# Channel mixes with 64-row contractions in pairs, and other places for the adds of x, in a convolution with a phase mixer

## The chip, the cores and the metric

The kernel runs on one core of a Trainium2 chip. The metric is the time of one execution on the device in microseconds (us). TensorE (PE in the profile, PEld for its weight loads), VectorE (DVE), ScalarE (ACT), GpSimd (POOL) and SyncE (SP) each run their own queue in order and wait for one another by semaphores; DMAs are issued from the queues of SP, ACT and POOL.

## The reference

```python
# x: (8, 4224, 192), weight: (8 heads, 7 taps); w_theta, w_ch: (192, 192); w_tok_r, w_tok_i: (4224, 4224)
w = softmax(weight, axis=-1)
x = causal convolution of x over the tokens, head h of 24 channels with the taps w[h]
theta = x @ w_theta
zr, zi = x * cos(theta), x * sin(theta)
y = einsum('ts,bsd->btd', w_tok_r, zr) + einsum('ts,bsd->btd', w_tok_i, zi)
u = x + y
return u + maximum(u @ w_ch, 0)
```

## The kernel before, in words

The token axis s of the two large products is cut into 33 chunks of 128 tokens (a chunk is four pieces of 32 tokens, a quarter of the sequence apart), the axis t of the results into 33 row blocks of 128. All 8 batches x 192 channels = 1536 columns are worked at once, in float16 with float32 sums.

**Chunks** (class `Chunk`). A chunk's tokens are loaded to `xw` (L194, GpSimd's queue; the history of 16 tokens comes by SP's queue from the chunk before, L185). `conv` multiplies with banded matrices `bands` on TensorE (L207). `transpose` turns the result on TensorE (L162). `theta` multiplies it with `wth` by `channel_mix` (L138) and takes cosine and sine on ScalarE (L243). `product` and `sums` on VectorE (L248, L254) form seven operands `z`, of which 11 chunks are held at a time. The convolved x also goes to DRAM (`xs`, L224).

**Channel mix** (L132 to L142). 192 channels need a contraction over 192 rows, and a transposed tile has 128. Three such tiles hold the channels of two batches. The weights stand in four columns of `wth` or `wch`, of which the middle two have one half of zeros: each batch takes two matmuls of 128 rows, the middle tile serving both. Per call (four batches) there are 8 matmuls of 192 columns. It is called 66 times for theta and 66 times for the final product with `wch`.

**Steps** (class `Step`). There are 58 steps. A step takes two row blocks (one, in the last unit) against the chunks that are active, up to 11. `mix` (L416) runs up to seven products over the chunks (two matmuls of 384 columns each, L429), a Strassen-like scheme that needs the weights of both row blocks and some sums of them. A unit of row blocks comes up about three times, 17 steps apart, once for each group of 11 chunks. In between, its sums `pv` lie in DRAM: `part` (stored at L442, loaded at L365 during the step before). VectorE adds each product from PSUM to `pv` (`give`, L394; in the first visits ScalarE copies, L392).

**Weights.** `load_w` loads the rows of w_tok_r and w_tok_i two steps ahead on GpSimd's queue (L316), into two buffers `st`. VectorE transposes them in 32x32 blocks (`turn`, L329) and sums them (`wsum`, L341), a step ahead of use.

**x in u = x + y.** Once per row block, x is added to `pv`. For 24 row blocks SP loads x to `xr` (one buffer, L375) and GpSimd adds it in place (L376), during the step before the one that uses `pv`, at 3.3 and 5.0 sevenths of it. For nine row blocks, those of the last five steps, GpSimd issues two DMAs each that add x to `part` in DRAM (L381), four steps ahead, in steps 49 to 53.

**Outputs.** After its last visit (steps 41 to 57) a row block is cast to float16 on ScalarE (`cast`, L451). In steps 41 to 52 a crossbar transfer turns it (`crossed`, L155, a transposing DMA on ScalarE's queue); in the last five, `late`, TensorE does (L162). `output` runs the channel mix, and VectorE adds the positive part (L464); SP stores.

**Order.** All order is written by hand. Each step has a list of events with a place in sevenths of the step (`step_events`, L501; `outputs`, L474, in us), and `mix` emits each when its place has come between two matmuls. Helpers `pe`, `dve`, `act` and `pool` keep each engine's instructions in the order of emission. At the start, the loop from L645 interleaves the first 11 chunks with the first steps.

Of the kernel before, what the change touches and what calls it, by code (L numbers as in the profile page):

```python
# [9 lines left out]
AT = mybir.ActivationFunctionType  # L10
ALU = mybir.AluOpType
F16 = mybir.dt.float16
F32 = mybir.dt.float32
# [3 lines left out]
def kernel(  # L17
# [52 lines left out]
    NOSYNC = mybir.DependencyInfo(  # L70
        mybir.DependencyClass.NoSync, mybir.DependencyReason.DATA
    )
    last = {}

    def in_order(engine, ins):
# [17 lines left out]
    constp = ctx.enter_context(tc.tile_pool(name="const", bufs=1))  # L93
    wk = ctx.enter_context(tc.tile_pool(name="wk", bufs=2))
# [22 lines left out]
    bands = constp.tile([2 * WR, H, 2, Q], F16, name="bands")  # L117
    ident = constp.tile([P, P], F16, name="ident")
    R = D - P
    wth = constp.tile([P, 4, D], F16, name="wth")  # L120
    wch = constp.tile([P, 4, D], F16, name="wch")

    def channel_pieces(w):

        return ((slice(0, P), 0, w[0:P, :]), (slice(0, R), 1, w[P:D, :]),
                (slice(R, P), 2, w[0:R, :]), (slice(0, P), 3, w[R:D, :]))

    def token(k, a):

# [1 line left out]

    def channel_mix(tT, w):  # L132

        v = banks("v")
        for k in range(2):
            for b in range(2):
                for i in range(2):
                    pe(nc.tensor.matmul(  # L138
                        v[:, k, b * D : (b + 1) * D], lhsT=tT[:, 3 * k + b + i, :],
                        rhs=w[:, 2 * b + i, :], start=(i == 0), stop=(i == 1),  # L140
                    ))
        return v[:, :, 0 : 2 * D]  # L142

    def evacuate(out, in_, by_dve=False):
        if by_dve:
            dve(nc.vector.tensor_copy(out=out, in_=in_))
        else:
            act(nc.scalar.activation(out=out, in_=in_, func=AT.Copy))  # L148
# [25 lines left out]
    class Chunk:  # L174
# [56 lines left out]

        def theta(self, g):
            v = channel_mix(self.xT[:, 6 * g : 6 * g + 6, :], wth).rearrange(
                "p k (b h e) -> p k b h e", b=2, h=2
            )
# [46 lines left out]
    class Step:  # L282


        def __init__(self, t):
            self.t, self.u, self.ks = t, unit(t), active(t)
            self.n = len(self.ks)
            self.tbs = [tb for tb in (2 * self.u, 2 * self.u + 1) if tb < NT]
            self.pair = len(self.tbs) == 2
            self.first = t < NU  # L290
            self.final = t + NU >= NSTEP
            self.late = self.final and self.n < NW
            self.ahead = self.late or 0 <= t + NU - NSTEP < 2
            visits = [v for v in range(NU, NSTEP) if v % NU == t % NU]
            self.adds = []
            for i, tb in enumerate(self.tbs):
                at = [v for v in visits if self.known(tb) < v - 1 and v + NU < NSTEP
                      and NU + 1 + base[-1] < v <= 2 * NU]
                at = at[0] if at else visits[-1]
                if t == at:  # L300
                    self.adds.append(i)
            self.time = 0.324 * self.n * (7 if self.pair else 4)
            self.st, self.w, self.ub, self.uT, self.pv = {}, {}, {}, {}, []

        def known(self, tb):

# [51 lines left out]
        def load_rows(self):  # L358
            for tb in self.tbs:
# [7 lines left out]
                    )  # L367
                self.pv.append(pv)

        def add_x(self, i):  # L370

            rows = slice(self.tbs[i] * P, (self.tbs[i] + 1) * P)
            if not self.ahead:
                xr = wk.tile([P, N], F16, name="xr", tag="xr", bufs=1)
                nc.sync.dma_start(out=xr, in_=xs[rows, :])  # L375
                pool(nc.gpsimd.tensor_tensor(  # L376
                    out=self.pv[i], in0=self.pv[i], in1=xr, op=ALU.add
                ))
                return
            for cols in (slice(0, HN), slice(HN, N)):  # L380
                pool(nc.gpsimd.dma_start(  # L381
                    out=part[(self.t // NU - 1) % 2][self.tbs[i], :, cols],
                    in_=xs[rows, cols], accum_op=ALU.add,
                ))

        def give(self, y, i, h, copies):
# [59 lines left out]
        def cast(self, i, g):  # L446
            if g == 0:
                self.ub[i] = wk.tile([P, N], F16, name="ub", tag="ub", bufs=2)
                self.uT[i] = turned()
            cols = slice(g * GC, (g + 1) * GC)  # L450
            act(nc.scalar.activation(  # L451
                out=self.ub[i][:, cols], in_=self.pv[i][:, cols], func=AT.Copy
            ))

        def turn_u(self, i, g):
            transposed(self.uT[i], self.ub[i], [g])
# [44 lines left out]
    def step_events(t):  # L501
        found = []
        s = steps[t]
        if t + 1 < NSTEP:
            found += steps[t + 1].w_tasks()
            found.append((1.6, steps[t + 1].load_rows))
            if not steps[t + 1].ahead:
                for i in steps[t + 1].adds:
                    found.append((3.3 + 1.7 * i, lambda i=i: steps[t + 1].add_x(i)))
        for s in steps[t:]:  # L510
            if s.ahead and t == s.t - (4 if s.late else 10):
                for i in s.adds:
                    found.append((3.3 + 1.7 * i, lambda s=s, i=i: s.add_x(i)))
        if t + 2 < NSTEP:
            nxt = steps[t + 2]
            for m in (1, 2):
                found.append((1.3 + 3 * (m - 1), lambda m=m: nxt.load_w(m)))
        for at, f in outputs:
            begin = at - sum(s.time for s in steps[:t])
            if 0 <= begin < steps[t].time:  # L520
                found.append((7 * begin / steps[t].time, f))
        if t >= NU - 2:
            new = [k for k in range(NK) if start[k] == t + 2 and k >= NW]
            for k in new:
                found.append((4.5, lambda k=k: load_chunk(k)))
            at = 0.1
            for k in (k for k in range(NK) if start[k] == t + 1 and k >= NW):
                pos = [0, .5, 1.4, 2.2, 2.6, 3.1, 3.15, 3.4, 3.6]

                def add(at, j, k):  # L530
                    def go():
                        if j == 0:
                            chunks[k].todo = chunks[k].tasks()
                        next(chunks[k].todo)()
                    found.append((at, go))
                for j, p in enumerate(pos):
                    add(at + p, j, k)
                at += 2.3
        return found


    load_chunk(0)
    stage = [wk.tile([P, 2, D], F32, name="stage", tag="ub", bufs=2) for _ in range(2)]
    for i in range(2):
        nc.vector.memset(stage[i][:, 1 - i, :], 0.0)
    for rows, i, part_w in channel_pieces(moe_w_theta):
        nc.sync.dma_start(out=stage[i // 2][rows, i % 2, :], in_=part_w)
    noise = zpool.tile([P, BH], F16, name="noise", tag="z")
    nc.vector.memset(noise, 0.0)
    sel = constp.tile([KS, Q - 1 + 2 * WR], F16, name="sel")  # L550
# [63 lines left out]
    act(nc.scalar.activation(  # L614
        out=bands[:, :, 1, :], in_=bv, func=AT.Copy, scale=block[:, 1:2]
    ))
    for i in range(2):
        dve(nc.vector.tensor_copy(out=wth[:, 2 * i : 2 * i + 2, :], in_=stage[i]))


    def stream():
# [18 lines left out]
    for m in (1, 2):  # L640
        steps[0].load_w(m)
    load_chunk(2)
    for m in (1, 2):
        steps[1].load_w(m)
    for i in range(NW + 2):  # L645
# [39 lines left out]
        if old:  # L685
            old.sums(1)
        between(1)
    dve(nc.vector.memset(wch[:, 1:3, :], 0.0))
    for rows, i, part_w in channel_pieces(moe_w_ch):
        nc.gpsimd.dma_start(out=wch[rows, i, :], in_=part_w)  # L690
    ready[0] = NK
# [33 lines left out]
```

## Time and profile before

| What | us |
|---|---|
| median of 20 runs | 1460.67 |
| lowest and highest of them | 1450.28, 1468.71 |
| the profiled execution | 1457.11 |
| its span in the profile | 1455.3 |
| crossbar transfers, 24: shortest, median, longest time to landing | 3.2, 7.3, 19.6 |
| DRAM adds of x, 18: shortest, median, longest time to landing | 5.4, 8.6, 20.2 |
| GpSimd adds of x, 24: mean of one | 3.11 |
| sums of weights, L341, 128x1408, 136: mean of one | 1.20 |

The profile is of one execution. Busy times of matmuls overlap, since each is counted to its modelled end; the pace is read from their starts. A line of a group gives the source line, the engine, the operation, what it writes and reads, the count, its busy time and the mean duration in ns; then the engine's idle time before such instructions and what ended it. A line of a timeline begins with the start in us and the busy time; consecutive instructions of one kind are merged. A line of a stage gives the busy time of each engine in it, with the number of instructions in brackets, then the clock that TensorE was granted (1.00 is full), the busy share of the DMA engines and GB/s. The step times are about 25 us with 11 chunks and two row blocks.

### The profile page before, as it was taken

The page shows a single profiled execution, that of the slowest core. Times are in us where ns is not written, and L with a number is a line of the kernel's source. Part 1 is how long each engine was busy: PE and PEld are TensorE (multiplying, and loading weights), DVE is VectorE, ACT ScalarE, POOL GpSimd, SP SyncE. Part 2 cuts the span into 40 slices and gives each one's busy share as a digit, 9 for nine tenths or more (in the row PEclk, how much of TensorE's full clock was granted, in tenths as well). Part 3 has the DMA queues.
Part 4 walks back from the last instruction along what each step waited for, and adds up shares of the span by engine and source line. Part 5 has one row for each costly group of instructions (what it writes and reads, how often), then busy time and mean ns, then how long its engine had stood idle before and what let it go on. Part 6 is the DMA issues. An engine that isn't in the chain of part 4 may idle for free.

```text
span 1455.3 us, 23744 instructions
## 1 busy us (share of the span) xinstructions
PE 1418.2 (97%) x9809; PEld 887.7 (61%) x9809; DVE 1014.7 (70%) x1048; ACT 317.6 (22%) x382; POOL 435.7 (30%) x655
## 2 busy tenths in 40 slices
PE   7899999999999999999999999999999999999997
PEld 4556666666666666666656556666666666666565
DVE  6894554555458687777777757877788688677585
ACT  5861101011134243000000004335100100100134
POOL 8421211111223322532322443232133124233220
PEclk9999999999999999999999999999999999999999
DMA  9985766564699999997878889999889999999983
GB/s 175 236 169 137 145 122 128 101 149 92 154 226 214 228 227 241 208 261 152 247 160 205 211 148 258 210 207 243 204 180 211 208 199 218 237 253 203 239 224 121
DMA packets 272028, 281.98 MB, mean 194 GB/s; under 512 B 106672, under 2 KB 240176, under 8 KB 271920
## 3 DMA queue, kind: packets, MB, share of 16 engines
q0 software_dynamic: 162464, 92.15, 48.3%
q1 hardware_dynamic: 71824, 178.88, 35.2%
q10 hardware_dynamic: 37632, 9.44, 4.5%
q8 instruction: 77, 1.26, 0.4%
q14 instruction: 31, 0.25, 0.1%
HBM read 245.49 MB, written 108.13 MB: 243 GB/s over the span
## 4 chain that ended last, share of the span: by engine, by line
PE 87%; DVE 5%; DMA 3%; ACT 3%; issue 1%; SPq 0%; DVEq 0%; POOL 0%; ACTq 0%; POOLq 0%
PE y L429 79%; PE v L138 5%; DVE wt L341 2%; PE pc L207 2%; PE tp L162 1%; DMA uT<-ub 1%; ACT z L243 1%; DVE pv L394 1%; DVE wt L329 1%; DVE z L254 1%; DMA pv<-part 1%; DVE z L248 0%; ACT uT L148 0%; DVE pv L464 0%; ACT pv L392 0%
## 5 line engine op out<-in xcount | busy, mean ns | idle before, releaser
L429 PE MATMUL y<-z,wt 128*128 128x384 f16 x7656 | 1285.8, 326 | 13.5 <-DVE pv L394 10.2
L429 PEld LDWEIGHTS <-wt 128*128 128x128 f16 x7656 | 741.4, 98 | 493.2 <-issue 16.0
L394 DVE TENSOR_TENSOR pv<-y,pv 128x768 f32<-128x768 f32 x324 | 308.5, 953 | 300.5 <-PE y L429 261.0
L329 DVE STREAM_TRANSPOSE wt<-st 128x1408 f16<-128x1408 f16 (+7 forms) x224 | 327.8, 1465 | 46.3 <-PE y L429 39.1
L316 POOL DMA_DIRECT2D st<-in_moe_w_tok_r_dram x232 | 132.8, 579 | 466.0 <-DVE wt L329 447.9
L316 POOL DMA_DIRECT2D st<-in_moe_w_tok_i_dram x232 | 132.8, 579 | 459.3 <-DVE wt L329 442.5
L341 DVE TENSOR_TENSOR wt<-wt 128x1408 f16<-128x1408 f16 (+7 forms) x216 | 215.7, 998 | 41.0 <-PE y L429 38.6
L148 ACT ACTIVATE z<-pc 128x768 f16<-128x768 f32 x65 | 53.3, 820 | 389.9 <-PE pc L207 389.7
L451 ACT ACTIVATE ub<-pv 128x768 f16<-128x768 f32 x66 | 52.5, 835 | 345.3 <-DVE pv L394 332.5
L392 ACT ACTIVATE pv<-y 128x768 f32<-128x768 f32 x66 | 54.0, 819 | 281.8 <-PE y L429 281.8
L138 PEld LDWEIGHTS <-uT 128*128 128x128 f16 x1056 | 90.9, 98 | 29.4 <-issue 7.7
L194 POOL DMA_DIRECT2D xw<-in_x_dram x132 | 76.3, 585 | 29.7 <-DMA xw<-xw 8.6
L464 DVE SCALAR_TENSOR_TENSOR pv<-v,pv 128x768 f32<-128x768 f32 x66 | 62.8, 953 | 26.5 <-PE v L138 25.0
L376 POOL TENSOR_TENSOR pv<-pv,xr 128x1536 f32<-128x1536 f32 x24 | 74.7, 3114 | 21.6 <-issue 19.2
L254 DVE TENSOR_TENSOR z<-z 128x768 f16<-128x768 f16 x132 | 73.4, 556 | 3.6
L148 ACT ACTIVATE uT<-tp 128x1536 f16<-128x1536 f16 (+1 forms) x48 | 58.3, 1216 | 66.2 <-PE tp L162 66.2
L243 ACT ACTIVATE z<-v,half_pi 128x768 f16<-128x768 f32 x66 | 59.9, 907 | 40.9 <-PE v L138 40.5
L248 DVE TENSOR_TENSOR z<-z 128x1536 f16<-128x1536 f16 x66 | 60.0, 948 | 7.0 <-ACT z L243 7.0
L138 PE MATMUL v<-wch,uT 128*128 128x192 f16 x528 | 54.9, 248 | 5.0 <-DMA uT<-ub 3.1
L138 PE MATMUL v<-wth,uT 128*128 128x192 f16 x528 | 54.4, 246 | 4.5 <-ACT z L243 3.0
L243 ACT ACTIVATE z<-v 128x768 f16<-128x768 f32 x66 | 53.5, 810 | 0.0
L207 PE MATMUL pc<-xw,bands 96*64 96x192 f16 x528 | 35.2, 255 | 3.1 <-DMA xw<-in_x_dram 1.5
(43 smaller groups left out, 140.0 us busy)
## 6 DMA issues: line engine op xcount, KB each, us to landing
part<-pv SPq DMA_DIRECT2D x79, 768.0 KB, 4.3
pv<-part SPq DMA_DIRECT2D x79, 768.0 KB, 6.3
out_dram<-pv SPq DMA_DIRECT2D x66, 384.0 KB, 4.6
st<-in_moe_w_tok_r_dram POOLq DMA_DIRECT2D x136, 176.0 KB, 5.7
st<-in_moe_w_tok_i_dram POOLq DMA_DIRECT2D x136, 176.0 KB, 4.7
xs<-z SPq DMA_DIRECT2D x132, 96.0 KB, 4.5
xw<-in_x_dram POOLq DMA_DIRECT2D x121, 96.0 KB, 6.1
xr<-xs SPq DMA_DIRECT2D x24, 384.0 KB, 4.5
```

The costliest lines, as they stand in the source:

```text
L138: pe(nc.tensor.matmul(v[:, k, b * D : (b + 1) * D], lhsT=tT[:, 3 * k + b + i, :], rhs=w[:, 2 * b + i, :], start=(i == 0), stop=(i == 1),))
L148: act(nc.scalar.activation(out=out, in_=in_, func=AT.Copy))
L194: nc.gpsimd.dma_start(out=self.xw[lo : lo + n, h, :, :], in_=x[:, t0 : t0 + n, :].rearrange("b s d -> s b d"),)
L207: pe(nc.tensor.matmul(pc[half * 2 * Q : (half + 1) * 2 * Q, h // 2, h % 2 * B * G : (h % 2 + 1) * B * G], lhsT=bands[:, 4 * j + h, :, :].r ...
L243: act(nc.scalar.activation(**args))
L254: dve(nc.vector.tensor_tensor(out=z[:, o, :], in0=z[:, a, :], in1=z[:, b, :], op=ALU.subtract))
L316: pool(nc.gpsimd.dma_start(out=st[a * Q : (a + 1) * Q, 0:nb, :, 0:n] .rearrange("i r bt s -> i (r bt) s"), in_=w[self.tbs[0] * P : (self.t ...
L329: dve(nc.vector.transpose(self.w[name][:, 0 : self.n, :, :], self.st[int(name[1])][:, int(name[0]) - 1, :, 0 : self.n * Q] .rearrange("p b ...
L341: dve(nc.vector.tensor_tensor(out=self.w[name][:, 0 : self.n, :, :], in0=self.w[a][:, 0 : self.n, :, :], in1=self.w[b][:, 0 : self.n, :, : ...
L376: pool(nc.gpsimd.tensor_tensor(out=self.pv[i], in0=self.pv[i], in1=xr, op=ALU.add))
L394: dve(nc.vector.tensor_tensor(out=o, in0=yv, in1=o, op=ALU.add))
L429: pe(nc.tensor.matmul(y[cn][:, q, 0:BH], lhsT=self.w[wn][:, c, :, :].rearrange("p bt i -> p (bt i)"), rhs=chunks[k].z[:, zn, q * BH : (q + ...
```

## The change

The channel mix keeps three columns of weights instead of four, without zeros. Per pair of batches it runs two matmuls over 128 rows (each batch's own tile), and then two over 64 rows: rows 0 to 63 of the middle tile for one batch, rows 64 to 127 for the other. Matmuls of 64 rows are issued as tiles of 64x128, at rows 0 and 64 of the array; the two results lie in different PSUM banks. The order of batches within the PSUM tile is therefore changed, and the cast before the final product permutes batches to suit.

The DRAM adds of the nine last row blocks move: for five of them to steps 27, 29 and 31 (into the partial sums of an earlier visit), for four to step 41. The GpSimd adds stay in the same steps; the load of x comes at 2 and 4 sevenths, the add at 3.6 and 5.6, and each add waits for the VectorE instruction that was emitted last before it. In the last two steps the first cast of each row block goes to VectorE. Chunk 3 is loaded before the weights of step 1. The memsets of the zero halves go.

```diff
+    SYNC = mybir.DependencyInfo(
+        mybir.DependencyClass.Sync, mybir.DependencyReason.SCHED_ONLY
+    )
...
-    wth = constp.tile([P, 4, D], F16, name="wth")
-    wch = constp.tile([P, 4, D], F16, name="wch")
+    wth = constp.tile([P, 3, D], F16, name="wth")
+    wch = constp.tile([P, 3, D], F16, name="wch")
...
         return ((slice(0, P), 0, w[0:P, :]), (slice(0, R), 1, w[P:D, :]),
-                (slice(R, P), 2, w[0:R, :]), (slice(0, P), 3, w[R:D, :]))
+                (slice(R, P), 1, w[0:R, :]), (slice(0, P), 2, w[R:D, :]))
...
         v = banks("v")
         for k in range(2):
-            for b in range(2):
-                for i in range(2):
-                    pe(nc.tensor.matmul(
-                        v[:, k, b * D : (b + 1) * D], lhsT=tT[:, 3 * k + b + i, :],
-                        rhs=w[:, 2 * b + i, :], start=(i == 0), stop=(i == 1),
-                    ))
+            for half in range(2):
+                pe(nc.tensor.matmul(
+                    v[:, half, k * D : (k + 1) * D], lhsT=tT[:, 3 * k + 2 * half, :],
+                    rhs=w[:, 2 * half, :], start=True, stop=False,
+                ))
+            for half, rows in enumerate((slice(0, R), slice(R, P))):
+                pe(nc.tensor.matmul(
+                    v[:, half, k * D : (k + 1) * D], lhsT=tT[rows, 3 * k + 1, :],
+                    rhs=w[rows, 1, :], start=False, stop=True,
+                ))
         return v[:, :, 0 : 2 * D]
...
-            self.ahead = self.late or 0 <= t + NU - NSTEP < 2
             visits = [v for v in range(NU, NSTEP) if v % NU == t % NU]
-            self.adds = []
+            quiet = [v for v in visits if start[2 * NW - 1] < v <= 2 * NU]
+            self.adds, self.ahead = [], []
             for i, tb in enumerate(self.tbs):
-                at = [v for v in visits if self.known(tb) < v - 1 and v + NU < NSTEP
-                      and NU + 1 + base[-1] < v <= 2 * NU]
-                at = at[0] if at else visits[-1]
-                if t == at:
+                known = self.known(tb)
+                if t not in ([v for v in quiet if known < v - 1] or visits[-1:])[:1]:
+                    continue
+                if not self.late:
                     self.adds.append(i)
+                else:
+                    far = known <= start[2 * NW - 1]
+                    self.ahead.append((i, 2 * NU - NW + 2 * (t % NU) if far else start[-1],
+                                       (t // NU - 1 - far) % 2))
...
         def add_x(self, i):
+            ins = pool(nc.gpsimd.tensor_tensor(
+                out=self.pv[i], in0=self.pv[i], in1=self.xr[i], op=ALU.add
+            ))
+            tc.add_manual_dep(ins.ins, last["dve"].ins.name, SYNC, reason="pace")
+
+        def add_ahead(self, i, which):
+            tb = self.tbs[i]
             for cols in (slice(0, HN), slice(HN, N)):
                 pool(nc.gpsimd.dma_start(
-                    out=part[(self.t // NU - 1) % 2][self.tbs[i], :, cols],
-                    in_=xs[rows, cols], accum_op=ALU.add,
+                    out=part[which][tb, :, cols], in_=xs[tb * P : (tb + 1) * P, cols],
+                    accum_op=ALU.add,
                 ))
...
-            act(nc.scalar.activation(
-                out=self.ub[i][:, cols], in_=self.pv[i][:, cols], func=AT.Copy
-            ))
+            evacuate(
+                self.ub[i][:, cols].rearrange("p (k h d) -> p h k d", h=2, d=D),
+                self.pv[i][:, cols].rearrange("p (h k d) -> p h k d", h=2, d=D),
+                self.t >= NSTEP - 2 and g == 0,
+            )
...
-            if not steps[t + 1].ahead:
-                for i in steps[t + 1].adds:
-                    found.append((3.3 + 1.7 * i, lambda i=i: steps[t + 1].add_x(i)))
-        for s in steps[t:]:
-            if s.ahead and t == s.t - (4 if s.late else 10):
-                for i in s.adds:
-                    found.append((3.3 + 1.7 * i, lambda s=s, i=i: s.add_x(i)))
+            for i in steps[t + 1].adds:
+                found.append((2 + 2 * i, lambda i=i: steps[t + 1].load_x(i)))
+                found.append((3.6 + 2 * i, lambda i=i: steps[t + 1].add_x(i)))
+        here = [(r, i, which) for r in steps for i, when, which in r.ahead if when == t]
+        for j, (r, i, which) in enumerate(here):
+            found.append((1.5 + 1.8 * j, lambda r=r, i=i, which=which: r.add_ahead(i, which)))
...
-    for i in range(2):
-        dve(nc.vector.tensor_copy(out=wth[:, 2 * i : 2 * i + 2, :], in_=stage[i]))
+    dve(nc.vector.tensor_copy(out=wth, in_=stage))
...
     load_chunk(2)
+    load_chunk(3)
     for m in (1, 2):
         steps[1].load_w(m)
...
-    dve(nc.vector.memset(wch[:, 1:3, :], 0.0))
     for rows, i, part_w in channel_pieces(moe_w_ch):
         nc.gpsimd.dma_start(out=wch[rows, i, :], in_=part_w)
```

More of the change, by code (lines that the diff above doesn't have):

```diff
@@ L233, in theta @@
             v = channel_mix(self.xT[:, 6 * g : 6 * g + 6, :], wth).rearrange(
-                "p k (b h e) -> p k b h e", b=2, h=2
+                "p b (k h e) -> p k b h e", k=2, h=2
             )
@@ L292, in __init__ @@
             self.late = self.final and self.n < NW
-            self.ahead = self.late or 0 <= t + NU - NSTEP < 2
             visits = [v for v in range(NU, NSTEP) if v % NU == t % NU]
-            self.adds = []
+            quiet = [v for v in visits if start[2 * NW - 1] < v <= 2 * NU]
+            self.adds, self.ahead = [], []
             for i, tb in enumerate(self.tbs):
-                at = [v for v in visits if self.known(tb) < v - 1 and v + NU < NSTEP
-                      and NU + 1 + base[-1] < v <= 2 * NU]
-                at = at[0] if at else visits[-1]
-                if t == at:
+                known = self.known(tb)
+                if t not in ([v for v in quiet if known < v - 1] or visits[-1:])[:1]:
+                    continue
+                if not self.late:
                     self.adds.append(i)
+                else:
+                    far = known <= start[2 * NW - 1]
+                    self.ahead.append((i, 2 * NU - NW + 2 * (t % NU) if far else start[-1],
+                                       (t // NU - 1 - far) % 2))
             self.time = 0.324 * self.n * (7 if self.pair else 4)
-            self.st, self.w, self.ub, self.uT, self.pv = {}, {}, {}, {}, []
+            self.st, self.w, self.xr, self.ub, self.uT, self.pv = {}, {}, {}, {}, {}, []
         def known(self, tb):
@@ L368, in load_rows, with load_x @@
                 self.pv.append(pv)
-        def add_x(self, i):
[L372 to L377, printed above, removed]
-                ))
-                return
+        def load_x(self, i):
+            self.xr[i] = wk.tile([P, N], F16, name="xr", tag="xr", bufs=1)
+            nc.sync.dma_start(
+                out=self.xr[i], in_=xs[self.tbs[i] * P : (self.tbs[i] + 1) * P, :]
+            )
+        def add_x(self, i):
+            ins = pool(nc.gpsimd.tensor_tensor(
[4 more added lines that the diff above has]
+            tb = self.tbs[i]
             for cols in (slice(0, HN), slice(HN, N)):
                 pool(nc.gpsimd.dma_start(
-                    out=part[(self.t // NU - 1) % 2][self.tbs[i], :, cols],
-                    in_=xs[rows, cols], accum_op=ALU.add,
+                    out=part[which][tb, :, cols], in_=xs[tb * P : (tb + 1) * P, cols],
+                    accum_op=ALU.add,
                 ))
@@ L450, in cast @@
             cols = slice(g * GC, (g + 1) * GC)
-            act(nc.scalar.activation(
-                out=self.ub[i][:, cols], in_=self.pv[i][:, cols], func=AT.Copy
-            ))
+            evacuate(
+                self.ub[i][:, cols].rearrange("p (k h d) -> p h k d", h=2, d=D),
+                self.pv[i][:, cols].rearrange("p (h k d) -> p h k d", h=2, d=D),
+                self.t >= NSTEP - 2 and g == 0,
+            )
         def turn_u(self, i, g):
@@ L542 @@
     load_chunk(0)
-    stage = [wk.tile([P, 2, D], F32, name="stage", tag="ub", bufs=2) for _ in range(2)]
-    for i in range(2):
-        nc.vector.memset(stage[i][:, 1 - i, :], 0.0)
+    stage = wk.tile([P, 3, D], F32, name="stage", tag="ub", bufs=2)
     for rows, i, part_w in channel_pieces(moe_w_theta):
-        nc.sync.dma_start(out=stage[i // 2][rows, i % 2, :], in_=part_w)
+        nc.sync.dma_start(out=stage[rows, i, :], in_=part_w)
     noise = zpool.tile([P, BH], F16, name="noise", tag="z")
@@ L616 @@
     ))
-    for i in range(2):
-        dve(nc.vector.tensor_copy(out=wth[:, 2 * i : 2 * i + 2, :], in_=stage[i]))
+    dve(nc.vector.tensor_copy(out=wth, in_=stage))
     def stream():
```

## The prediction

> **What bounds the kernel now.** I read the page first (busy shares, then the chain of waits), then the stages of the span with their clock, then the timeline around each thing that the diff touches. The page and its chain:
>
> ```profile
> PE 1418.2 (97%) x9809; PEld 887.7 (61%) x9809; DVE 1014.7 (70%) x1048; ACT 317.6 (22%) x382; POOL 435.7 (30%) x655
> PE 87%; DVE 5%; DMA 3%; ACT 3%; issue 1%; SPq 0%; DVEq 0%; POOL 0%; ACTq 0%; POOLq 0%
> L138 PE MATMUL v<-wch,uT 128*128 128x192 f16 x528 | 54.9, 248 | 5.0 <-DMA uT<-ub 3.1 <-DVE pv L464 1.1 <-ACT uT L148 0.5
> ```
>
> TensorE is the bound: 97% busy, 87% of the chain. So what a part is worth is the TensorE time that it adds or takes, plus the stalls of TensorE that it removes. Idle TensorE is 1455.3 - 1418.2 = 37 us. The timeline of TensorE shows the pace of matmuls (start to start; busy times overlap):
>
> ```profile
> 430.72 0.33 PE L429 MATMUL y<-z,wt 128*128 128x384 f16 x1
> 430.97 0.52 PE L207 MATMUL pc<-xw,bands 96*64 96x192 f16 x8
> 431.43 2.77 PE L429 MATMUL y<-z,wt 128*128 128x384 f16 x16
> 436.98 0.82 PE L138 MATMUL v<-wth,uT 128*128 128x192 f16 x8
> 437.64 1.14 PE L429 MATMUL y<-z,wt 128*128 128x384 f16 x6
> ```
>
> A channel mix (L138) holds TensorE from 436.98 to 437.64: 0.66 us for 8 matmuls, 82.5 ns each. The convolution (L207) is the only user of a divided array: 64 output columns each, two side by side. Its 8 matmuls cost more than four times 82.5 ns = 330 ns. It starts 250 ns after the L429 before it, where L429 follows L429 after 162, and the next L429 comes 460 ns after its start. In the single records, in all 56 such places to within a few ns: 256 ns into the convolution (93 over 163), members of a pair 3 to 4 ns apart, 107 ns to the second pair (24 over 83), 182 ns from the last pair to L429 (99 over 83), 173 ns to the L429 after that (10 over 163). One excursion into the divided array and back costs 93 + 24 + 99 + 10 = 226 ns.
>
> The one long stall of TensorE in the steady part:
>
> ```profile
> 1329.49 5.32 ACTq L155 DMA_TRANSPOSE uT<-ub  x1
> 1335.40 1.76 POOL L381 DMA_DIRECT2D part<-xs  x2
> 1349.17 1.46 PE L138 MATMUL v<-wch,uT 128*128 128x192 f16 x8 [3.12 <-DMA uT<-ub]
> ...
> 1329.49 19.64 DMA uT<-ub
> ...
> 1349.00:1351.00 2.00, 1.83 (x10) 1.49 (x11) 0.26 (x1) 0.00 (x0) 1.16 (x2) 0.50 1.16 261
> 1351.00:1356.00 5.00, 5.00 (x24) 2.77 (x23) 1.36 (x2) 0.00 (x0) 1.69 (x2) 0.60 1.26 253
> ```
>
> A crossbar transfer issued at 1329.49 takes 19.64 us (the median of the 24 is 7.3), with adds of x in DRAM (L381) beside it. The mix waits 3.1 us, and the columns after the busy times give a granted clock of 0.50 and 0.60 afterwards (clock record: half speed for 6.8 us).
>
> A slow sum of weights:
>
> ```profile
> 802.43 4.49 DVE L341 TENSOR_TENSOR wt<-wt 128x1408 f16<-128x1408 f16 x1
> 803.05 3.12 POOL L376 TENSOR_TENSOR pv<-pv,xr 128x1536 f32<-128x1536 f32 x1
> 809.37 2.92 PE L429 MATMUL y<-z,wt 128*128 128x384 f16 x17 [0.76 <-DVE pv L394]
> ```
>
> The sum takes 0.88 us by the median; beside a GpSimd add it takes 4.49, and TensorE waits 0.76 us a little later.
>
> **What the Trainium skill says.** "TensorEngine Tiling (Array Packing)", Tiling Modes, lists 64x128 as a mode of two tiles and says that changing the mode, not just the tile, drains TensorE. The trace agrees for the 128x64 mode (93 and 99 ns of lost pace at the two edges); nothing in it runs a 64x128 tile between full ones. The same page, Restrictions, says that column tiling switches off the fast weight load; row tiling isn't named there. "TensorE: Matmul & The Clock Gate", Part 3, has tiles of one mode running together with starts 4 ns apart, as the 3 to 4 ns here. "SBUF — State Buffer", Who interferes with whom, describes one port pair that VectorE and GpSimd take in turn for whole instructions; 4.49 beside 0.88 us agrees.
>
> **The change part by part.**
>
> *Channel mixes.* Still 8 matmuls, but per k two full ones, then two of 64 rows, one in each half of the array and writing different banks. So F F P F F P, with P a pair. Saved: each pair runs in one slot, 82.5 - 4 = 79 ns, twice a call: 158 ns. Added: the mode changes into and out of each pair, two excursions a call, four edges. No trace shows this mode's price. Lower bound: nothing, if only the column division drains; upper: the whole 226 ns of the convolution. I take 215, since the page says that any change of mode drains, and the 24 ns at the first pair may be the slower weight load of 64 columns, of which I leave half. A call then costs 2 x 215 - 158 = +272 ns, 0.93 us in place of 0.66. There are 66 + 66 = 132 calls: +35.9 us. Cover: 22 calls lie in the first 110 us, where VectorE and ScalarE share the chain. L138 is 7.1% of that chain, 7.8 us, while 22 calls of 0.82 are 18 us, so about 43% are on the path and 22 x 0.272 x 0.57 = 3.4 us are hidden. The 19 calls after 1382 us are on the chain (14.7% of it) and count in full. Sum: +32.5 us.
>
> *Adds in DRAM.* 18 issues for nine row blocks move from steps 49 to 53 to earlier ones: five blocks to steps 27, 29 and 31, four to step 41. GpSimd's queue then carries 2 to 4 more issues of about 1.0 us (L381's mean) in each of the former and eight in step 41, in front of loads of weights. Those loads waited 890 us in all for a free buffer, so an issue earlier or later is covered; uncovered, it delays a transpose of weights by a few us, once a step. The last adds of step 41 are issued about as its end, at 1049 us, and so meet the first two crossbar transfers, which landed in 3.4 us for a mix at 1062: 10 us of slack. Removed: the 3.1 us wait and the half of 6.8 us lost to the clock, 6.5 us together. Next late there is nothing: the other transfers landed in 3.2 to 9.5 us.
>
> *GpSimd adds.* Each of the 24 now waits for VectorE's last instruction before it, at 3.6 and 5.6 sevenths of a step, a sum at 3.3 or 5.1. Behind it on GpSimd stand the loads of weights, with the slack just told; SP's second load of x (4.0) waits for the first add's end, about 4.5: half of a seventh of 25 us, 1.8 us, before stores that are not waited for. TensorE's waits for VectorE between 110 and 1020 us are 3.9 us in five places, three of them beside such adds (0.76, 0.82, 0.82): -2.4 us. Sums stretched elsewhere were hidden already.
>
> *Start.* Chunk 3 is loaded before the weights of step 1, on GpSimd's queue. At 27.82 us a convolution waits 1.5 us for its x. Two memsets go from the start (0.42 us of VectorE, not on the path) and one of 0.22 us from VectorE's busy stretch at 102.7, where TensorE waits 2.5 us. Since ScalarE and VectorE carry the chain here and the weights come later, I take -1.2 us of the 1.7, and bound it by +1 and -2.
>
> *Casts.* Three of 0.83 us leave ScalarE for VectorE, which did a similar cast in 0.96; in the last 10 us two casts in a row (1.58 us) become parallel: -0.5 us, between 0 and -1.2. The permuted reading of the others keeps 768 elements: no cost.
>
> Sum: 32.5 - 6.5 - 2.4 - 1.2 - 0.5 = +21.9. The profiled execution took 1457.1 (span 1455.3), so 1479. The median of the 20 is 1460.7, and its spread from 1450 to 1469 looks like such crossbar stalls in different numbers, which this change takes away: a floor of 1450.3 less the other gains (4.1), plus 32.5, gives 1478.7. I predict **1480 us**.
>
> **Rivals.** (1) *The row division doesn't drain*: weights for one half load beside work in the other, and partial sums need not leave first. Then each call loses 158 ns, with cover as above about -19 us; with -10.6 of the rest, 1460.7 - 30 = 1431, faster. For it: the convolution's price could belong to its column division and slow weight load. Against: the weight loads there begin only with the matmul, 91 ns after the stream before has ended, and the same happens on the way back, where the load is of the ordinary kind. The point from which it decides: with the other gains at 10.6, break-even is +80 ns a call, that is four edges worth 238, 60 ns an edge against 113 in the convolution. (2) *A half price*, 40 to 60 ns an edge: between 2 and 82 ns a call, 1450 to 1460. (3) *The pairs do not run side by side* (the same bank or order holds them): +158 ns more a call, about +20 us, 1500. Against: banks differ, and the convolution's pairs do. (4) *The crossbar stall stays*, because loads of weights and not the adds delayed the transfer: +6.5 on the likeliest, 1486.
>
> **How the numbers follow.** The likeliest case, edges of 75 to 115 ns, has 0.65 and its own range 1465 to 1492; with (4) inside it. (3) has 0.04, (2) 0.12, (1) 0.19. The range 1442 to 1494 takes in the likeliest and the half price, and leaves out (1) and (3). About 0.2% (3 us) is what a measurement can tell from no change. Faster: 0.19 and most of (2), 0.28; same 0.04; slower 0.68.
>
> **What would show it.** Right: four gaps of about 90 ns in each channel mix, calls of 0.87 to 0.95 us from first start to the next L429, TensorE's busy time up by some 30 us; no wait for a crossbar transfer near 1349, full clock throughout; sums of weights never above 2 us beside adds. Wrong: 64-row matmuls whose neighbours keep an 82.5 ns pace, calls of 0.50 us. Then the price of the edge was mis-sized.

## The result and the profile after

The changed kernel takes 1476.75 us (median of 7 runs, 1475.77 to 1479.9); the kernel before took 1459.14 us in runs of the same time (48 runs, 1450.28 to 1468.82). The ratio is 1.0124, 95% interval 1.0098 to 1.0149: slower by some 17.6 us. The profiled execution took 1478.1 us with a span of 1476.3.

First the page of the changed kernel: busy times, the chain, and from the list of groups the weight loads of the 64-row matmuls (L146; L141 are the 128-row ones; L448 is what L429 was, and these matmuls of the two large products are called L-matmuls here). An edge is a change of tile shape from one matmul to the next; an excursion goes into the 64-row tiles and back, over two edges.

```profile
PE 1450.0 (98%) x9809; PEld 855.9 (58%) x9809; DVE 979.8 (66%) x1047; ACT 316.1 (21%) x379; POOL 435.3 (29%) x655
PE 91%; DMA 3%; DVE 3%; ACT 1%; issue 1%; SPq 0%; POOL 0%; DVEq 0%; ACTq 0%
L146 PEld LDWEIGHTS <-uT 64*128 64x128 f16 x528 | 25.3, 93 | 42.1 <-issue 42.1
```

TensorE has the same 9809 matmuls and is busy 32 us longer (1450.0 against 1418.2), while its share of the chain grew from 87% to 91%. Before the weight loads of the 64-row tiles, weight loading stood idle for 42.1 us, put down to "issue": no semaphore held them. That is 80 ns for each of the 528, or 160 before each pair. The timeline of matmuls and loads in one mix shows how the loads lie:

```profile
1371.64 0.26 PEld L141 LDWEIGHTS <-uT 128*128 128x128 f16 x2
1371.80 0.33 PE L141 MATMUL v<-wch,uT 128*128 128x192 f16 x2
1372.06 0.10 PEld L146 LDWEIGHTS <-uT 64*128 64x128 f16 x2 [0.16 <-issue]
1372.06 0.26 PE L146 MATMUL v<-wch,uT 64*128 64x192 f16 x2
1372.25 0.11 PEld L141 LDWEIGHTS <-uT 128*128 128x128 f16 x2
1372.25 0.34 PE L141 MATMUL v<-wch,uT 128*128 128x192 f16 x2
```

The first loads begin 0.16 us ahead of their matmuls, the others together with theirs, both on the way into the 64-row tiles and on the way back. So at an edge the loads are not fetched ahead as they are within one shape. A load takes 92 or 98 ns (medians of 64-row and full tiles), about as much as an edge will turn out to cost; that the price is this load, no longer hidden, was not tested.

The timeline of TensorE, two channel mixes of the changed kernel; columns are start, busy time, instruction, and the count of those merged:

```profile
440.98 0.33 PE L141 MATMUL v<-wth,uT 128*128 128x192 f16 x2
441.24 0.26 PE L146 MATMUL v<-wth,uT 64*128 64x192 f16 x2
441.43 0.34 PE L141 MATMUL v<-wth,uT 128*128 128x192 f16 x2
441.70 0.26 PE L146 MATMUL v<-wth,uT 64*128 64x192 f16 x2
441.88 1.15 PE L448 MATMUL y<-z,wt 128*128 128x384 f16 x6
```

From 440.98 to 441.88 a mix now holds TensorE for 0.91 us in the single records, where it was 0.66. Two full matmuls need 0.165 us of pace, but 0.26 pass before the pair starts; the pair needs 0.083, but 0.19 pass before full ones come again. In the single records the starts follow each other by 82, 178, 3, 185, 93, 178, 3 and 185 ns, then 173 to the second L448, each the same within 2 ns in at least 113 of the 119 mixes that stand between two L448.

The crossbar transfers and the sums of weights, from the views of their lines (L163, L353), and a GpSimd add in the timeline of the changed kernel:

```profile
L163 ACTq DMA_TRANSPOSE uT<-ub x24: 1290/1652/5107, 1060.7 to 1380.1; - x24
DMA to landing us min/median/max: 3.6/6.4/9.4
...
L353 DVE TENSOR_TENSOR wt<-wt x216: 291/881/2612, 15.7 to 1438.6; 128x1408 f16<-128x1408 f16 x68, 128x1152 f16<-128x1152 f16 x22, 128x512 f16<-128x512 f16 x4, 128x896 f16<-128x896 f16 x4
...
814.16 1.80 DVE L353 TENSOR_TENSOR wt<-wt 128x1408 f16<-128x1408 f16 x2
816.09 3.10 POOL L391 TENSOR_TENSOR pv<-pv,xr 128x1536 f32<-128x1536 f32 x1 [4.89 <-issue]
816.82 0.96 DVE L413 TENSOR_TENSOR pv<-y,pv 128x768 f32<-128x768 f32 x1 [0.86 <-PE y L448]
```

The longest transfer fell from 19.6 to 9.4 us and no mix waits for one. The longest sum fell from 4.59 to 2.61 us: the add at 816.09 starts after the two sums, not beside them. The one of 2.61 us, at 621.07, still lies beside an add, which began at 619.84: an add waits for the VectorE instruction before it, but the next sum can start while it runs. TensorE did not wait there. These two parts of the change work as meant; the mix takes more than they give.

### The profile page after: what moved, and what is told of

It is laid out like the page before. It is cut to its first block, busy times and chain, and to the rows that moved or that the text cites. A ratio compares the mean times of both kernels' runs of the same rounds, so it can differ in the third digit from the quotient of the medians.

```text
span 1476.3 us, 23744 instructions
## 1 busy us (share of the span) xinstructions
PE 1450.0 (98%) x9809; PEld 855.9 (58%) x9809; DVE 979.8 (66%) x1047; ACT 316.1 (21%) x379; POOL 435.3 (29%) x655
## 4 chain that ended last, share of the span: by engine, by line
PE 91%; DMA 3%; DVE 3%; ACT 1%; issue 1%; SPq 0%; POOL 0%; DVEq 0%; ACTq 0%
PE y L448 81%; PE v L141 4%; PE v L146 3%; PE pc L215 2%; PE tp L170 1%; DMA xw<-xw 1%; ACT z L251 1%; DVE pv L413 1%; DVE z L262 1%; DMA pv<-part 1%; DMA st<-in_moe_w_tok_r_dram 1%; DVE z L256 0%; DVE pv L485 0%; DMA xw<-in_x_dram 0%; DVE wt L341 0%
## 5 line engine op out<-in xcount | busy, mean ns | idle before, releaser
L448 PE MATMUL y<-z,wt 128*128 128x384 f16 x7656 | 1285.2, 326 | 8.7 <-DVE pv L413 6.0
L448 PEld LDWEIGHTS <-wt 128*128 128x128 f16 x7656 | 732.8, 98 | 497.5 <-issue 9.1
L353 DVE TENSOR_TENSOR wt<-wt 128x1408 f16<-128x1408 f16 (+7 forms) x216 | 175.8, 814 | 40.8 <-PE y L448 38.2
L202 POOL DMA_DIRECT2D xw<-in_x_dram x132 | 76.3, 585 | 26.7 <-DMA xw<-xw 6.2
L141 PEld LDWEIGHTS <-uT 128*128 128x128 f16 x528 | 40.5, 98 | 39.1 <-issue 9.1
L146 PEld LDWEIGHTS <-uT 64*128 64x128 f16 x528 | 25.3, 93 | 42.1 <-issue 42.1
L141 PE MATMUL v<-wth,uT 128*128 128x192 f16 x264 | 44.8, 252 | 4.9 <-ACT z L251 2.5
L141 PE MATMUL v<-wch,uT 128*128 128x192 f16 x264 | 44.1, 249 | 1.8 <-DVE pv L485 1.1
```

The costliest lines, as they stand in the source:

```text
L141: pe(nc.tensor.matmul(v[:, half, k * D : (k + 1) * D], lhsT=tT[:, 3 * k + 2 * half, :], rhs=w[:, 2 * half, :], start=True, stop=False,))
L146: pe(nc.tensor.matmul(v[:, half, k * D : (k + 1) * D], lhsT=tT[rows, 3 * k + 1, :], rhs=w[rows, 1, :], start=False, stop=True,))
L202: nc.gpsimd.dma_start(out=self.xw[lo : lo + n, h, :, :], in_=x[:, t0 : t0 + n, :].rearrange("b s d -> s b d"),)
L353: dve(nc.vector.tensor_tensor(out=self.w[name][:, 0 : self.n, :, :], in0=self.w[a][:, 0 : self.n, :, :], in1=self.w[b][:, 0 : self.n, :, : ...
L448: pe(nc.tensor.matmul(y[cn][:, q, 0:BH], lhsT=self.w[wn][:, c, :, :].rearrange("p bt i -> p (bt i)"), rhs=chunks[k].z[:, zn, q * BH : (q + ...
```

## The experiments

All times are medians of runs interleaved with runs of the kernel before; that had 1460.0 us beside e1 to e4 and 1459.4 beside e5 to e8.

**The mix alone** (e1). The kernel before with the new `channel_mix`, three columns of weights and the permuted cast, no other part:

```diff
...
+            for half, rows in enumerate((slice(0, R), slice(R, P))):
+                pe(nc.tensor.matmul(
+                    v[:, half, k * D : (k + 1) * D], lhsT=tT[rows, 3 * k + 1, :],
+                    rhs=w[rows, 1, :], start=False, stop=True,
+                ))
```

> The kernel before with the changed channel mix alone (and what it needs: three columns of weights, the permuted cast). Theory (each edge between the full array and 64-row tiles costs about 100 ns, four edges a call, 158 ns saved by two pairs): a mix takes 0.91 us from its first start to the next L-matmul in place of 0.66, 132 calls cost 34 us, some 3 us hidden at the start: +31 us, 1490 us, ratio 1.021. Rival (a good part of the slower mix is covered, and the rest of the change gives nothing): +18 us, 1477 us, ratio 1.012.

Measured: 1481.45 us (1479.9 to 1483.3), ratio 1.0135 (1.0093 to 1.0176). The mixes have the starts shown above to within 1 ns, 0.91 us each, as the theory says, but the total is 8.5 us less than it said. The view of this kernel's transfers and its waits of TensorE from 1020 to 1400 us give the likely reason:

```profile
DMA to landing us min/median/max: 3.2/6.7/12.2
...
PE v L138 <- ACT uT L153: 0.6, 2, 0.3
PE v L138 <- ACT z L248: 0.4, 1, 0.4
PE y L434 <- DVE pv L399: 0.3, 1, 0.3
```

The DRAM adds still lie beside the transfers here, and yet the longest takes 12.2 us and TensorE waits for none. The stall that the kernel before has did not come, so this run is to be set against a kernel without it (e4 below): 1481.45 - 1451.63 = 29.8 us. The theory's 31 is met within 1.2. Why the stall stays away with the slower mix (other places of the DMAs in time, or more time for them) was not tried.

**All but the mix** (e2). The changed kernel with the old mix, and so with four columns of weights and casts that do not permute:

```diff
...
+            for b in range(2):
+                for i in range(2):
+                    pe(nc.tensor.matmul(
+                        v[:, k, b * D : (b + 1) * D], lhsT=tT[:, 3 * k + b + i, :],
+                        rhs=w[:, 2 * b + i, :], start=(i == 0), stop=(i == 1),
```

> The changed kernel with the old channel mix (128-row matmuls with zero halves): all parts but the mix. Theory: the other parts give what the mix alone does not explain, 31 - 18 = 13 us: 1446 us, ratio 0.991; no long wait for a crossbar transfer, no sum of weights near 4 us. Rival (the other parts give nothing, the mix costs only 18): 1459 us, ratio 1.000.

Measured: 1450.04 us (1448.2 to 1452.75), ratio 0.9937 (0.9912 to 0.9962). The other parts together give 10.0 us; set against the changed kernel, the mix costs 1476.75 - 1450.04 = 26.7 us, or 28.2 in the two profiled spans (1476.3 and 1448.1). Both halves of the rival fall. The other parts give 3 us less than the theory took, which had them from the total less 31. No mix waits for a transfer (the longest takes 10.3 us), and the longest sum takes 2.60 us.

**One excursion instead of two** (e3). All 128-row matmuls of a call first, then both pairs:

```diff
-                    rhs=w[:, 2 * half, :], start=True, stop=False,
+                    rhs=w[:, 2 * half, :], start=(k == 0), stop=False, skip_group_check=True,
                 ))
+        for k in range(2):
             for half, rows in enumerate((slice(0, R), slice(R, P))):
...
-                    rhs=w[rows, 1, :], start=False, stop=True,
+                    rhs=w[rows, 1, :], start=False, stop=(k == 1), skip_group_check=True,
```

The second pair of batches (k = 1) has no start flag of its own here, since it shares its banks with the first, whose sums are still open.

> The changed kernel with the mix in the order F F F F P P: the four 128-row matmuls first, then the two pairs, so one excursion into 64-row tiles a call instead of two. Theory (the edges are the price): a call takes about 0.71 us instead of 0.91, 132 calls with some cover give -24 us against the changed kernel: 1453 us, ratio to before 0.996. Rival (the pairs are slow for another reason, as their banks or their dependence on the sums just written): no change, 1477 us, ratio 1.012.

Measured: 1452.72 us (1450.02 to 1454.82), ratio 0.9952 (0.9933 to 0.997): 24.0 us less than the changed kernel. The timeline:

```profile
440.05 0.49 PE L141 MATMUL v<-wth,uT 128*128 128x192 f16 x4
440.47 0.34 PE L147 MATMUL v<-wth,uT 64*128 64x192 f16 x4
440.74 1.15 PE L449 MATMUL y<-z,wt 128*128 128x384 f16 x6
```

A call takes 0.697 us in the single records (440.05 to 440.74). Taking away two of the four edges takes away 0.21 us, with the same 8 matmuls and the same pairs. What is left is still above the 0.66 of the old mix: one excursion costs more than the two pairs save.

**Twice the edges** (e7). Each 64-row matmul behind its own 128-row one:

```diff
-            for half in range(2):
+            for half, rows in enumerate((slice(0, R), slice(R, P))):
                 pe(nc.tensor.matmul(
...
-            for half, rows in enumerate((slice(0, R), slice(R, P))):
                 pe(nc.tensor.matmul(
```

(In the text that follows, H is a single matmul of 64 rows.)

> The changed kernel with each 64-row matmul behind its own 128-row one (F H F H F H F H): no pairs, eight edges a call instead of four. Theory (an edge costs 100 ns wherever it stands): a call takes about 1.46 us from its first start to the next L-matmul instead of 0.91, +67 us over the changed kernel: 1544 us, ratio 1.058. Rival (the drain is paid once a call, or depends on pairs): a call of 1.07 us (two slots more, as the pairs are split), +20 us: 1497 us.

Measured: 1553.77 us (1552.59 to 1555.17), ratio 1.0638 (1.0598 to 1.0678): 77 us more than the changed kernel, 10 more than expected.

```profile
438.20 0.25 PE L141 MATMUL v<-wth,uT 128*128 128x192 f16 x1
438.37 0.25 PE L145 MATMUL v<-wth,uT 64*128 64x192 f16 x1
438.56 0.26 PE L141 MATMUL v<-wth,uT 128*128 128x192 f16 x1
...
439.68 0.50 PE L447 MATMUL y<-z,wt 128*128 128x384 f16 x2
```

A call takes 1.487 us in the single records. Against the 0.910 of the changed kernel that is 0.577 more, of which two more slots are 2 x 0.079 = 0.158; the remaining 0.42 over four edges are 105 ns an edge. 132 calls make 76 us of it, so hardly anything is covered, where the theory had reckoned with some cover and a call of 1.46. So the price is paid at every change of shape, not once a call, and whether the 64-row matmuls come in pairs or alone.

**Only the DRAM adds** (e4). The kernel before with the adds in steps 27, 29, 31 and 41:

```diff
-        for s in steps[t:]:
-            if s.ahead and t == s.t - (4 if s.late else 10):
...
+        here = [(r, i, which) for r in steps for i, when, which in r.ahead if when == t]
+        for j, (r, i, which) in enumerate(here):
```

> The kernel before with only the DRAM adds of x moved to steps 27, 29, 31 and 41. Theory (the adds beside the crossbar transfers delay them): no transfer over 10 us, no wait of TensorE for one, no half clock there, -6 to -8 us: 1452 us, ratio 0.995, and the runs spread less than those of before. Rival (loads of weights delay the transfers): 1459 us, ratio 1.000, transfers near 20 us remain.

Measured: 1451.63 us (1450.33 to 1453.79), ratio 0.9936 (0.9912 to 0.996), 8.4 us less. The spread of its 16 runs is 3.5 us, where that of before is 16 us or more in each of its three sets of runs; the fastest of before (1450.28) and of this kernel (1450.33) are the same. The view of the transfers in this kernel, then the stage around the old stall, first in the kernel before, then in this one (columns as told under "Time and profile before"):

```profile
DMA to landing us min/median/max: 3.2/6.8/9.8
...
1330.00:1360.00 30.00, 26.88 (x164) 16.62 (x163) 16.08 (x17) 1.58 (x2) 8.16 (x12) 0.89 1.27 202
...
1330.00:1360.00 30.00, 30.00 (x203) 19.08 (x201) 19.94 (x21) 3.15 (x4) 4.88 (x9) 1.00 0.89 191
```

TensorE is busy throughout at full clock, where the kernel before has 26.88 of 30 us at a mean clock of 0.89. The adds delayed the transfer, not the loads of weights: both profiles issue the transfer (1329.49 and 1329.44), the load of `pv` after it (1331.05 and 1330.95) and four loads of weights (from 1333.06 and 1333.01) at the same times, and to landing these take 19.6, 17.9 and 16 to 18 us before, 8.7, 7.4 and 5.6 here. What is gone here are the pairs of adds from 1325.51 and 1335.40. Four of the moved adds still lie beside the first two transfers, as forecast, and these are the longest here: 9.8 and 9.6 us, for which no mix waits.

**The GpSimd adds held, on top of e4** (e5):

```diff
...
+            tc.add_manual_dep(ins.ins, last["dve"].ins.name, SYNC, reason="pace")
...
-                found.append((3.3 + 1.7 * i, lambda i=i: steps[t + 1].add_x(i)))
+                found.append((2 + 2 * i, lambda i=i: steps[t + 1].load_x(i)))
+                found.append((3.6 + 2 * i, lambda i=i: steps[t + 1].add_x(i)))
```

> The kernel with only the DRAM adds moved (1451.6 us), and the GpSimd adds held behind the sums of weights as in the change. Theory (adds stretched sums of weights to over 4 us and TensorE waited some 0.8 us in two or three places): -2 us, 1449.5 us, ratio to before 0.993; no wait of TensorE for VectorE between 700 and 850 us. Rival (the wait for VectorE delays GpSimd's loads of weights and gives it back): 1451.6 us or more.

Measured: 1449.82 us, ratio 0.9925 (0.9895 to 0.9955), 1.8 us less than e4; the intervals overlap. The waits of TensorE for VectorE from 110 to 1020 us, first in e4, then in this kernel:

```profile
PE y L434 <- DVE pv L399: 3.0, 4, 0.8
```

```profile
PE y L441 <- DVE pv L406: 1.5, 2, 0.7
```

Two of four waits went (those at 709 and 810 us), 1.5 us: the size of the gain, though the two profiled spans differ by 0.9 only. The two that stay lie at 494 and 944 us, where no GpSimd add runs.

**Chunk 3 first, on top of e4** (e6):

```diff
     load_chunk(2)
+    load_chunk(3)
```

> The kernel with only the DRAM adds moved, and chunk 3 loaded before the weights of step 1. Theory of the prediction (a convolution no longer waits for its x): -1.2 us, 1450.4 us. Rival (ScalarE and VectorE carry the start, and the weights of step 1 come later): no change or slower, 1451.6 to 1452.5 us.

Measured: 1452.18 us (1450.12 to 1455.33), ratio 0.9943 (0.9923 to 0.9964): no gain, if anything 0.5 us slower. The convolution at 26.45 us no longer waits for its x (0.9 us in e4), but the mix after it waits 0.9 us for ScalarE:

```profile
26.45 0.59 PE L207 MATMUL pc<-xw,bands 96*64 96x192 f16 x8
27.94 0.82 PE L138 MATMUL v<-wth,uT 128*128 128x192 f16 x8 [0.90 <-ACT z L148]
```

Still, about half of the gain is there at first: this mix starts at 27.94 us, in e4 at 28.43, and an L-matmul follows at 34.05, in e4 at 34.54. It is lost later in this profile. TensorE has half its clock from 103.64 to 107.05 us, where e4 has the full one, and at 634.59 it waits 0.82 us for VectorE, whose sum at 627.59 took 4.55 us beside a GpSimd add; e4 has no wait there. So the rival's number came, but not by the rival's reason alone, and what the start is worth by itself was not resolved.

**One excursion for two calls** (e8). All other parts of the change. The mixes of both halves of a chunk or row block are put together, eight 128-row matmuls and then four pairs; at the start and in the last five steps the old mix stays. The weights keep four columns, whose inner two serve both forms.

```diff
+        vs = [banks("v") for _ in range(NG)]
+        for g, v in enumerate(vs):
+            for k in range(2):
+                for half in range(2):
...
+                        rhs=w[:, 3 * half, :], start=(k == 0), stop=False,
...
+        for g, v in enumerate(vs):
+            for k in range(2):
+                for half, rows in enumerate((slice(0, R), slice(R, P))):
...
+                        rhs=w[rows, 1 + half, :], start=False, stop=(k == 1),
```

> All other parts of the change, with the mixes of both halves of a chunk or row block put together where they can be: eight 128-row matmuls, then four pairs, one excursion for two calls; at the start and in the last five steps the old 128-row mix. The second chunk of a step starts 0.7 sevenths later. Theory (one excursion of about 200 ns against four pairs that save 79 ns each): two calls in 1.21 us instead of 1.32, 46 times, -4 to -5 us against the old mix with the other parts (1450.0): 1445.5 us, ratio 0.990. Rival (two PSUM tiles at once hold up TensorE or VectorE): 1450 us or more.

Measured: 1444.6 us (1443.44 to 1446.53), ratio 0.9891 (0.9861 to 0.9921), the fastest of all, 5.4 us under e2 (3.3 between the profiled spans, 1448.1 and 1444.8).

```profile
441.48 0.82 PE L153 MATMUL v<-wth,uT 128*128 128x192 f16 x8
442.23 0.51 PE L162 MATMUL v<-wth,uT 64*128 64x192 f16 x8
442.67 5.37 PE L470 MATMUL y<-z,wt 128*128 128x384 f16 x32
```

Two calls in 1.19 us (441.48 to 442.67) in place of 1.32. With four pairs to one excursion the 64-row tiles pay. Something of the rival came too: from 110 to 1400 us TensorE waits for VectorE's adds to `pv` for 3.4 us, in e2 for 1.8; whether the two PSUM tiles or the shifted places are the cause was not tried.

## Why the prediction was right

*What bounds the kernel.* TensorE, and what was reckoned from its pace came out: nearly all that the mix adds shows in the end, apart from the start and the last stretch.

*The price of an edge.* The prediction took it from the convolution, which divides the array by columns, and this was the term with the largest doubt. I took 215 ns for an excursion; measured are 178 - 82.5 = 96 ns into the pair, 185 - 82.5 = 103 out of it, and 10 more at the second full matmul, some 208 together. The half of the 24 ns that I left for the slower weight load has no place in a mix with one pair to an excursion; where a second pair follows at once (e3, e8), it starts 93 ns after the first, 10 over 83. A call costs +260 ns (predicted 272): 910 for 660, and 10 more after it. The saving of a pair was reckoned as 79 ns and is 79 to 80. In the sum is a slip: the 99 ns on the convolution's way back are counted from the first member of the last pair and so hold the 4 ns between members already, which the saving of 79 leaves out once more. That is some 8 ns of the 12 a call.

Rival (1), no drain, and rival (2), half the price, fall by the starts alone; rival (3), no pairs side by side, by the 3 ns between the members. The edge is the cause, and not something else in the 64-row matmuls: half the edges gave back 24.0 us (e3, expected 24), twice the edges cost 77 us (e7, expected 67). Nor is it a wait for sums just written: in e8 all eight full matmuls come first, and the first pair still starts 178 ns after the last of them. What the array does at an edge, a drain as the prediction had it, no run shows; they show its price, and that the weight loads begin only with their matmuls there.

*The sum of the mixes.* 132 x 0.260 = 34.3 us, less cover. Predicted +32.5, measured +26.7 between the medians of e2 and after (28.2 between their profiles, 29.8 between e1 and e4). Counting L-matmuls in the single records of the changed kernel and e2, the 28.2 us fall into three stretches. Up to the 300th (119.5 and 118.3 us), 1.2 us show of 22 x 0.260 = 5.7; from there to the 7400th, 23.4 of 23.7 (91 calls); after it, 3.5 of 4.9, in the 19 calls that were to count in full. So the term was too large, on the profiles by 4.3 us: 1.6 by the price of a call, 1.1 by the start, 1.4 by the last stretch, the rest between. The number for the start is not cover alone, since the clock is in it: e2 has half its clock from 104.65 to 108.06 us, where the changed kernel has the full one, and before that, at the 200th L-matmul with the same 22 calls done, the changed kernel was 3.6 us behind, after a longer spell of half clock of its own (6.8 us from 38.09, 3.4 from 36.38 in e2). The 1.5 us between medians and profiles were not resolved.

*The DRAM adds.* Predicted -6.5, and the profiled span of e4 is 6.5 us shorter than that of before (1448.8 against 1455.3); the median gains 8.4, since the wide spread of before went too. Rival (4), loads of weights as the cause, falls by e4.

*The held adds.* Predicted -2.4, measured -1.8 (0.9 between the profiled spans). Sums beside an add fell from 17 in the kernel before to two. The sign that none of them takes over 2 us failed once, by the 2.61 at 621.07, for which TensorE did not wait.

*The start and the casts.* Predicted -1.2 within +1 and -2 for the start, measured about +0.5 in e6, where half a microsecond was won at first and lost elsewhere. Predicted -0.5 for the casts; e2 differs from e5 by the start and the casts and is 0.2 us slower, so the two together give nothing that can be measured.

*The sum.* On the profiled execution predicted +21.9 us, measured 1476.3 - 1455.3 = +21.0; in the median predicted 1480, measured 1476.75, which is +17.6. The nearness is luck in part. On the profiles the mix costs 28.2 us instead of 32.5, and the other parts give 7.2 (1455.3 - 1448.1) instead of 10.6: two terms too large, with opposite signs. The direction was not luck: it came from one comparison, two excursions of some 208 ns against two pairs of 79, and the starts show both. Full clock throughout, also forecast, did not come: near 1349 us the clock was full, but in the start it was half for 6.8 us (below).

## What to carry to other kernels

Count the changes of the array's shape, not only the matmuls that a division saves: here an excursion into 64-row tiles and back cost 208 ns, as much as 2.6 pairs of 192 columns saved. Two pairs to an excursion lost and four gained; that three would just pay is worked out from these figures, not measured. If the trace has another divided matmul, its gaps at both ends can serve as an estimate of the price: 226 ns in the convolution here, 208 in the mix. And a part can be worth more in the median than on one profile (8.4 and 6.5 us for the DRAM adds) when the kernel's runs spread and the part takes the spread away.

## What the hardware showed that I had not expected

DRAM adds beside crossbar transfers do not always delay them. Of the two profiles with the adds in steps 49 to 53, one has a transfer of 19.6 us (before) and the other none over 12.2 (e1). The runs of before lie between 1450 and 1469 us, while the kernel with the adds moved stays within 1450.3 and 1453.8, and the slower mix alone within 1479.9 and 1483.3 with the adds still in place. That the longer executions of before have such stalls and the shorter ones none is likely, but only one of them was profiled; what decides it is open.

A sum of weights on VectorE waits out a GpSimd add that runs beside it. In the kernel before, 16 of the 17 sums beside an add end 0.75 to 0.76 us after the add does, wherever they began; the other one overlaps the add by 0.17 us only and takes its usual 0.88. The transposes (9, 1.64 us) and the additions to `pv` from PSUM (13, 0.96 us) that run beside a GpSimd add take no longer than elsewhere. So of the VectorE instructions that met an add, only these sums had to be kept apart from it.

Changing the division by rows costs nearly what changing it by columns does: into the pairs 96 ns against 93, out of them 103 against 96, both counted from the matmul just before. Yet the convolution's weight loads of 64 columns take 109 ns by the median and those of the 64-row tiles 92.

TensorE's clock was granted at half for 6.8 us early on in the profile of the changed kernel (38 to 45 us) and for 3.4 us in that of e4 (from 39), but not there in the kernel before:

```profile
36.00:46.00 10.00, 8.69 (x59) 3.91 (x59) 6.97 (x13) 5.25 (x8) 5.96 (x11) 0.66 1.08 159
```

The stage from 36 to 46 us of the changed kernel has a clock of 0.66, where the kernel before has 1.00. Such spells come and go between these kernels: five of the ten profiles (e2, e3, e5, e6, e8) have one of 3.4 us near 105. There the cost can be read: from the 200th to the 300th L-matmul the two kernels with the old mix and no spell take 18.9 us (before, e4) and the three with one take 20.6 (e2, e5, e6), 1.7 us for 3.4 us at half clock. So a change of one microsecond in the start can't be told from one profile.
